# Sketched attention and a tanh-shrink feed-forward: a fixed order table in place of the scheduler

## The chip, the cores and the metric

The kernel runs on one core of a Trainium2 chip. The metric is the device time of one execution in microseconds, the median of three runs.

## The reference

```python
def _attn_ref(q, k, v, S1, S2):            # q, k, v: (4, 4, 1088, 32); S1, S2: (8, 32)
    def phi(x):
        a = np.einsum('rd,bhsd->bhsr', S1, x)
        b = np.einsum('rd,bhsd->bhsr', S2, x)
        return np.einsum('bhsi,bhsj->bhsij', a, b).reshape(*x.shape[:-1], r * r)
    q_p, k_p = (phi(q), phi(k))
    kv = np.einsum('bhsf,bhsd->bhfd', k_p, v)
    z = np.sum(k_p, axis=2)
    num = np.einsum('bhsf,bhfd->bhsd', q_p, kv)
    den = np.einsum('bhsf,bhf->bhs', q_p, z)[..., None] + 1e-06
    return (num / den)
...
def _moe_ref(x, w_in, w_out):              # x: (4352, 128); w_in: (128, 2048); w_out: (2048, 128)
    h = x @ w_in
    g = h - np.tanh(h)
    return (g @ w_out)
```

The attention output, with its four heads side by side, is `x`: 4 batches of 1088 tokens are 4352 rows of 128.

## The kernel before, in words

The kernel is written as a list of operations (`P.add`), each with the values it reads and writes and the engines that may run it. `schedule` then places them: it goes forward in planned time, takes on each engine the ready operation with the lowest key inside a short window, picks the buffer or PSUM bank that it uses, and puts fills into gaps of PE that it sees coming. A fill is a product of zeros (L435, the operand `zz` is cleared by the operation `zop` at L434) into a bank that is not read. `sync` derives the semaphore waits from the dependencies, and `emit` writes out the five instruction streams, each in its strict order.

**Attention, per batch b.** k and q come in from HBM. VectorE transposes k in 32 x 32 blocks (kT, L583, two instructions) and q (qT, L592). PE makes the k sketches (ksk, L599 for batch 0 and L610 for the others), VectorE transposes them back (kab, L616). PE forms a Gram product of the two sketches (L638), from which a weighted sketch column for the denominator is made (gm, L642; scmm, L625; sc, L648, into the operand `wq`). VectorE forms the outer products of the two k sketches (w, L659, three of 128 x 768), PE multiplies them with v (kvmm, L671); kvd, kvt (L703) and kvb bring the result into place. On the q side PE makes the sketch with `wq` (qsk, L724), VectorE transposes it (abc, L729), computes the denominator and divides (m, den, rd, ap, L741 to L749), forms the outer products (qp, L767) and transposes them (qpT, L772). PE multiplies with kvb (num, L783) and two copies (L375, a helper that serves ScalarE, VectorE and GpSimd) write bf16 columns of `xT`. Blocks are 128 tokens; batch 0 has its q side in pieces of 2, 3 and 4 blocks, batch 1 in 5 and 4, batches 2 and 3 in one piece of 9 each. x1.0 is the pair of copies for the first 5 blocks of batch 1.

**Feed-forward.** The 4352 columns of `xT` are cut into ten groups of 256, 384, 448, six times 512, and 192 columns; groups 0 to 2 are exactly batch 0. For each of 16 blocks of `w_in` PE computes h (L877) into one of three PSUM banks, ScalarE takes the tanh (L881), PE accumulates the output from it (o, L892). The linear part h @ w_out is carried by `wch` and `wcl`, a product of both weight matrices computed on the chip (L845, L855), two more products per group (L896). So a column passes PE 16 + 18 times. From group 7 on, the tanh covers two blocks at once. VectorE transposes the group's result (ot, L901), and SP stores it (L911), four or eight stores per group.

**Order.** The attention's keys put it ahead of the feed-forward; the feed-forward's keys rise with time. All loads are on SP's queue in the order of their keys, at most 1.4 MB ahead: k of batch 0 in two halves, part of q, v, the weights, then the other batches.

## Time and profile before

| | us |
|---|---|
| runs | 113.57, 113.77, 115.36; median 113.77 |
| span of the profiled execution, first to last instruction | 112.6 |
| median of the runs less that span (what lies around it) | 1.2 |
| PE / VectorE / ScalarE / GpSimd busy | 100.3 / 72.1 / 79.9 / 5.6 |
| first tanh starts | 20.03 |
| batch 1's first x copied, group 3 starts | 48.16, 48.45 |
| last product of PE ends | 108.86 |

The profile is one execution; its lines give start and duration in us, the engine, the line of the kernel, the operation, its output and input tiles, how many instructions are merged in the line, and in brackets how long the engine had waited and for what. DVE is VectorE, ACT ScalarE, POOL GpSimd, PE TensorE, PEld its weight loads. Ends of PE's instructions are modelled and overlap, so the spacing of starts tells its rate. The granted clock of TensorE is 0.998 over the span.

### The profile page before, as it was taken

What the parts mean: (1) busy time and instruction counts of PE and PEld (TensorE: products, weight loads), DVE (VectorE), ACT (ScalarE), POOL (GpSimd) and SP (SyncE); (2) the same over time, 40 slices, a digit from 0 to 9 for tenths busy, and PEclk for the clock granted to TensorE, in tenths of its full rate; (3) what the DMA queues carried; (4) which work ended last, traced back from release to release, by engine and by line L of the source; (5) the groups of instructions that cost most, each with busy time, mean ns of one, the idle gap of its engine ahead of it and who ended that gap; (6) DMA issues with size and microseconds to landing.
All of it is one profiled execution on the core that took longest, in us unless ns stands there. A gap on an engine that the chain in (4) does not pass through costs nothing.

```text
span 112.6 us, 3409 instructions
## 1 busy us (share of the span) xinstructions
PE 100.3 (89%) x1467; PEld 48.7 (43%) x1477; DVE 72.1 (64%) x115; ACT 79.9 (71%) x164; POOL 5.6 (5%) x25
## 2 busy tenths in 40 slices
PE   6975996998799989979999999979999999999960
PEld 4523783455355444436443346334243334334540
DVE  4469374899999999999999992499950020020030
ACT  2101247876487798586599867798969999999950
POOL 5202016000000000000000000000000000000000
PEclk9999999999999999999999999999999999999999
DMA  1999878799987804022000230005004106005035
GB/s 21 259 245 329 255 232 234 243 241 272 226 270 218 165 5 69 0 47 46 0 6 0 44 49 6 6 11 83 0 6 68 25 0 93 0 12 77 4 55 73
DMA packets 25037, 11.24 MB, mean 100 GB/s; under 512 B 18880, under 2 KB 23616, under 8 KB 25024
## 3 DMA queue, kind: packets, MB, share of 16 engines
q1 hardware_dynamic: 24320, 10.97, 40.7%
q8 instruction: 11, 0.18, 0.7%
q10 hardware_dynamic: 704, 0.08, 0.5%
q14 instruction: 2, 0.02, 0.1%
HBM read 8.81 MB, written 2.23 MB: 98 GB/s over the span
## 4 chain that ended last, share of the span: by engine, by line
PE 36%; ACT 28%; DVE 16%; DMA 13%; issue 2%; SPq 1%; DVEq 0%
ACT th L881 25%; PE psb L892 11%; PE psb L877 10%; DMA qL<-in_q_dram 5%; DMA wo_f<-in_moe_w_out_dram 5%; PE psb L783 5%; DVE qp L767 4%; DVE qpT L772 4%; DVE abc L729 3%; DMA kL<-in_k_dram 3%; PE psb L724 3%; PE psb L671 3%; DVE ot L901 2%; PE psb L610 2%; ACT wiT L375 2%
## 5 line engine op out<-in xcount | busy, mean ns | idle before, releaser
L881 ACT ACTIVATE th<-psb 128x512 bf16<-128x512 f32 (+4 forms) x136 | 69.5, 624 | 7.4 <-PE psb L877 6.6
L877 PE MATMUL psb<-xT,wi 128*128 128x512 bf16 (+4 forms) x155 | 50.1, 349 | 1.5 <-DVE xT L375 0.5
L892 PE MATMUL psb<-th,wo 128*128 128x512 bf16 (+4 forms) x157 | 48.2, 348 | 1.4 <-DVE ot L901 0.6
L877 PEld LDWEIGHTS psb<-xT,wi 128*128 128x128 bf16 x160 | 14.9, 97 | 25.3 <-ACT th L881 14.4
L892 PEld LDWEIGHTS psb<-th,wo 128*128 128x128 bf16 x160 | 14.6, 97 | 15.7 <-ACT th L881 7.5
L901 DVE STREAM_TRANSPOSE ot<-psb 128x512 f32<-128x512 f32 (+4 forms) x10 | 6.3, 626 | 22.6 <-PE psb L892 22.6
L772 DVE STREAM_TRANSPOSE qpT<-qp 128x768 f32<-128x768 f32 (+1 forms) x14 | 12.1, 861 | 0.4
L767 DVE TENSOR_TENSOR qp<-ap,abc 128x768 f32<-128x768 f32 (+1 forms) x14 | 11.5, 818 | 0.1
L659 DVE TENSOR_TENSOR w<-abk 128x768 f32<-128x768 f32 x12 | 11.3, 981 | 0.1
L729 DVE STREAM_TRANSPOSE abc<-psb 128x1152 f32<-128x1152 f32 (+2 forms) x5 | 5.7, 1143 | 5.1 <-PE psb L724 5.0
L435 PE MATMUL psb<-zz 128*128 128x256 bf16 x33 | 7.8, 388 | 1.1 <-DVE zz L434 1.1
L783 PE MATMUL psb<-qpT,kvb 32*32 32x128 f32 (+4 forms) x448 | 8.3, 309 | 0.1
L375 ACT CAST xT<-psb 128x192 bf16<-128x192 f32 (+4 forms) x8 | 3.3, 421 | 5.4 <-PE psb L783 5.4
L583 DVE STREAM_TRANSPOSE kT<-kL 128x576 f32<-128x576 f32 (+1 forms) x8 | 5.6, 724 | 1.7 <-DMA kL<-in_k_dram 1.7
L783 PEld LDWEIGHTS psb<-qpT,kvb 32*32 32x32 f32 x448 | 5.1, 103 | 2.9 <-DVE qpT L772 2.0
L671 PE MATMUL psb<-w,vL 128*32 128x64 f32 x288 | 6.0, 243 | 0.0
L592 DVE STREAM_TRANSPOSE qT<-qL 128x1088 f32<-128x1088 f32 (+2 forms) x5 | 5.3, 1055 | 0.9 <-DMA qL<-in_q_dram 0.9
L435 PEld LDWEIGHTS psb<-zz 128*128 128x128 bf16 x33 | 4.1, 135 | 3.6 <-DVE zz L434 1.1
L671 PEld LDWEIGHTS psb<-w,vL 128*32 128x32 f32 x288 | 5.1, 125 | 0.3 <-issue 0.2
L642 ACT COPY gm<-psb 128x32 f32<-128x32 f32 x4 | 0.8, 198 | 5.6 <-PE psb L638 5.6
L724 PE MATMUL psb<-qT,wq 32*32 32x288 f32 (+2 forms) x160 | 3.6, 381 | 0.9 <-ACT xT L375 0.9
L375 DVE CAST xT<-psb 128x192 bf16<-128x192 f32 (+3 forms) x6 | 2.8, 467 | 1.1 <-PE psb L783 1.0
(55 smaller groups left out, 56.6 us busy)
## 6 DMA issues: line engine op xcount, KB each, us to landing
kL<-in_k_dram SPq DMA_DIRECT2D x3, 544.0 KB, 3.6
qL<-in_q_dram SPq DMA_DIRECT2D x3, 544.0 KB, 4.9
vL<-in_v_dram SPq DMA_DIRECT2D x4, 288.0 KB, 4.8
vL<-in_v_dram SPq DMA_DIRECT2D x4, 256.0 KB, 5.0
wi_f<-in_moe_w_in_dram SPq DMA_DIRECT2D x4, 256.0 KB, 4.7
wo_f<-in_moe_w_out_dram SPq DMA_DIRECT2D x4, 256.0 KB, 5.8
out_dram<-ot SPq DMA_DIRECT2D x16, 64.0 KB, 2.0
out_dram<-ot SPq DMA_DIRECT2D x8, 56.0 KB, 1.9
```

The costliest lines, as they stand in the source:

```text
L375: return e.copy(o, i) if name == "scalar" else e.tensor_copy(o, i)
L435: filler = (lambda e, n: e.matmul(bank(3)[:, 0:256], zz.ap[:, 0:128], zz.ap[:, 128:384], start=True, stop=True), zop)
L659: P.add(_v(768), lambda e, n: e.tensor_tensor(out=wv.ap.rearrange("p (x i j) -> p x i j", i=8, j=8), in0=abh(0)[:, :, :, None].to_broadcas ...
L671: i = e.matmul(pv[b].ap[h * 32:(h + 1) * 32, 0:64], vL[b][:, h, blk * 32:(blk + 1) * 32], wvs[b, p].ap[:, (bi * 4 + h) * 64:(bi * 4 + h + ...
L729: P.add(_vp(sn * 4), lambda e, n: e.transpose(abc.ap.rearrange("p k h f -> p h k f")[:, :, 0:s1 - s0, :], psa4[:, :, 0:sn].rearrange("p h ...
L767: P.add(_v(cn * 256), lambda e, n, qp=qp, c0=c0, cn=cn: e.tensor_tensor(out=qp.ap[:, 0:cn * 256].rearrange("p (x i j) -> p x i j", i=8, j= ...
L772: P.add(_v(cn * 256), lambda e, n, qp=qp, o0=o0, cn=cn: e.transpose(qt.ap[:, o0 * 256:(o0 + cn) * 256], qp.ap[:, 0:cn * 256]), r=[qp], w=[ ...
L783: i = e.matmul(psa4[h * 32:(h + 1) * 32, g, 0:nb * 32], kvb.ap[g * 32:(g + 1) * 32, x, h * 32:(h + 1) * 32], qq[g * 32:(g + 1) * 32, 0:nb, ...
L877: P.add(_pe(n_ / 2.4 + 2.6), lambda e, n, jb=jb, hv=hv: e.matmul(hv.ap[:, jb % m * 512:jb % m * 512 + n_], wi[jb // 4].ap[:, (jb % 4) * 12 ...
L881: P.add(_a(n_ * m), lambda e, n, hv=hv, th=th: e.activation(out=th.ap.rearrange("p (u x) -> p u x", u=m)[:, :, 0:n_], in_=hv.ap.rearrange( ...
L892: fn = lambda e, n, x=x, st=st, sp_=sp_: e.matmul(ov.ap[:, 0:n_], wo[x // 4].ap[:, x % 4, :], ths[x][0].ap[:, ths[x][1] * 512:ths[x][1] * ...
L901: P.add(_vp(n_), lambda e, n: e.transpose(ot.ap[:, 0:n_], ov.ap[:, 0:n_]), r=[ov], w=[ot], key=-60000, name=f"ot{gi}")
```

## The change

The scheduler, its keys, windows and costs are gone. `TABLE` holds for every operation, by its number in the order of the `P.add` calls, the engine (v, a, g, t, s) and behind a colon the buffer or bank chosen; `f` is a fill. `plan` reads the table from front to back and appends each operation to its engine's list. `sync` and `emit` remain; an engine other than PE now also waits for its own earlier instructions where a buffer is reused, which before was done only where data was read.

```diff
+WPOOL = [False, True, True, True]
+TABLE = """
+42g 19s 18a 9g 15v 1g 20s 17a 44g 48g 21s 6g 46g 10g 8g 24s 7g 2g 23s 5v 27s 51v:0 52v 40v 28s 41v f f f f f f f f f f
+f f f f f f f f f f f f f 54t:0 0v 13v 22s 16v 53v 26s 4v 50g 25s 56v:0 43g 55v 3g f f f f f 57t:0 62v:0 32s 58a:0
...
+    def plan(self, table, filler):
...
+            if token == "f":
+                o = _Op()
+                o.engs, o.fn, o.mode, o.name, o.dma = {"tensor": 0}, filler[0], "128x128", "fill", 0
+                o.deps, o.users, o.vals, o.lock = {filler[1]: True}, [], [], False
+                e = "tensor"
...
-                            if d.eng == e and not (raw and e != "tensor"):
+                            if d.eng == e == "tensor":
...
-    zop = P.add(_v(192), lambda e, n: e.memset(zz.ap[:, :], 0.0), w=[zz], key=-99000)
+    zop = P.add(_v(192), lambda e, n: e.memset(zz.ap[:, :], 0.0), w=[zz], name="zz")
     filler = (lambda e, n: e.matmul(bank(3)[:, 0:256], zz.ap[:, 0:128], zz.ap[:, 128:384], start=True, stop=True), zop)
...
-    wqs = [sb("wq", [128, 32]) for _ in range(2)]
+    wqs = [sb("wq", [128, 32]) for _ in range(B)]
...
-    w_p = _Pool([([_Bank() for _ in range(3)], [sb("w", [128, 3 * 256]) for _ in range(3)])])
+    w_p = pool("w", 6, [128, 3 * 256])
...
+        P.add(_pe(80, 200.0), scmm, r=[s2r, gms[b]], w=[pg], mode="128x32", name=f"scmm{b}")
+        P.add(_a(8), lambda e, n: e.copy(wqs[b][:, 16:24], pg.ap[:, 64:72]), r=[pg], w=[scv[b]], name=f"sc{b}")
...
-        P.add(_v(768), lambda e, n: e.tensor_tensor(
+        P.add({**_v(768), **_g(768, 2.2)} if WPOOL[b] else _v(768), lambda e, n: e.tensor_tensor(
...
-            P.add(_pe(485), sk, r=[kT[b], wab], w=[pk[rh]], key=nk(), mode="64x32", name=f"ksk{b}.{rh}")
+        P.add(_pe(557, 245.0), sk, r=[kT[b], wab], w=pk, mode="64x32", name=f"ksk{b}")
```

Numbers that matter at the start: 0 is the memset of `zz`, 1, 2 and 3 make the identity, 4 and 5 the masks, 13 to 16 memsets of v's padding, 19 the load of k of batch 0, 40 and 41 `stt` and `wab` (the sketch operand), 51 and 52 the two k transposes of batch 0, 53 its first qT, 54 its k sketch, 55 and 56 kab, 57 the Gram product, 61 to 63 the outer products.

What the table and the diff set:

- VectorE's list begins 15, 5, 51, 52, 40, 41, 0, 13; PE's begins with 23 fills, then 54; 36 more fills lie between there and the fourth product of group 0. Before, 19 fills ran ahead of the first sketch and 33 in all.
- k of batch 0 is one load. The order on SP's queue: k0, first part of q0, first half of v0, two blocks of `w_in`, one of `w_out`, the rest of q0, and so on; up to 2.0 MB ahead. k and qT of batch 3 share batch 0's buffers.
- Outer products w1.0, w2.1 and w2.2 (batch, third) are on GpSimd, the other nine on VectorE. All casts of the weights but two are on ScalarE.
- VectorE does batch 0's second q front before its first qpT; then, between batch 0's q side and batch 1's, kT, kab and the outer products of batches 1 to 3 and all three qT. On PE the k products of batches 1 to 3 come before batch 1's q sketch. Both copies of x1.0 are on ScalarE.
- `wq` has one buffer per batch, and scmm is an operation of its own for every batch, in the Gram product's bank. The transposes of `w_in` and the products for `wch` are grouped by four into one operation.
- Tanh and products of a group no longer go in the order of the blocks. Stores are mostly issued a group or more later than they are ready.

## The prediction

> **What bounds the kernel now.** I read the whole-span table first, then the engine timelines, then the chain that ended last. The table gives each engine's busy share and, in 40 slices of 2.8 us, its busy tenths:

> ```profile
> PE 100.3 (89%) x1467; PEld 48.7 (43%) x1477; DVE 72.1 (64%) x115; ACT 79.9 (71%) x164; POOL 5.6 (5%) x25
> DVE  4469374899999999999999992499950020020030
> ACT  2101247876487798586599867798969999999950
> ```

> VectorE is full from slice 7 to 24 (17 to 67 us), ScalarE only from slice 30 on. PE's busy time overlaps itself, so I use the spacing of its starts. The stretches differ, so I read the timeline at their borders (start, duration, engine, line, operation):

> ```profile
> 0.84 0.22 DVE L434 MEMSET zz<- 128x192 uint32 x1 [0.84 <-PEq L976]
> 1.12 4.24 PE L435 MATMUL psb<-zz 128*128 128x256 bf16 x19 [1.12 <-DVE zz L434]
> 4.22 0.78 DVE L583 STREAM_TRANSPOSE kT<-kL 128x576 f32<-128x576 f32 x1 [1.71 <-DMA kL<-in_k_dram]
> 5.27 0.70 DVE L583 STREAM_TRANSPOSE kT<-kL 128x512 f32<-128x512 f32 x1
> 6.03 1.22 PE L599 MATMUL psb<-kT,wab 64*32 64x288 f32 x16 [0.67 <-DVE kT L583]
> 7.28 0.85 DVE L616 STREAM_TRANSPOSE abk<-psb 128x288 f32<-128x288 f32 x2
> 8.16 3.11 DVE L659 TENSOR_TENSOR w<-abk 128x768 f32<-128x768 f32 x3
> 9.70 0.76 POOL L375 CAST wi<-wi_f 128x512 bf16<-128x512 f32 x1 [4.16 <-DMA wi_f<-in_moe_w_in_dram]
> 20.03 4.53 ACT L881 ACTIVATE th<-psb 128x256 bf16<-128x256 f32 x16 [1.07 <-PE psb L877]
> 31.78 2.69 DVE L659 TENSOR_TENSOR w<-abk 128x768 f32<-128x768 f32 x3
> 47.67 0.49 DVE L375 CAST xT<-psb 128x320 bf16<-128x320 f32 x1
> 48.45 0.59 PE L877 MATMUL psb<-xT,wi 128*128 128x512 bf16 x2 [0.53 <-DVE xT L375]
> 103.04 0.38 PE L877 MATMUL psb<-xT,wi 128*128 128x512 bf16 x1
> 103.26 0.38 PE L892 MATMUL psb<-th,wo 128*128 128x512 bf16 x1
> 108.89 0.38 DVE L901 STREAM_TRANSPOSE ot<-psb 128x192 f32<-128x192 f32 x1 [1.29 <-PE psb L892]
> ```

> Three stretches follow. Up to 8.16 us (the first outer product) there is one chain: k load, two transposes, k sketch, its transposition. From there to 48.45 us VectorE sets the pace, with some 4 us of gaps before 20 us, until batch 1's first activations are copied (x1.0) and group 3, the first that needs them, can start. From 48.45 us PE is the bound: a 512-column product starts every 0.215 us (103.04 to 103.26, and so on). Groups 3 to 9 hold 3264 columns, each passing 16 + 18 times: 3264/512 x 34 x 0.215 = 46.6 us. The attention products in that stretch add 9.7 us, and each of their nine runs costs 0.33 us around it, as here in the chain that ended last (start, us, what):

> ```profile
> 65.90 1.53 PE psb L783 x63
> 67.43 0.16 issue
> 67.59 0.38 PE psb L896
> ```

> (0.16 without work, then a product that takes 0.38 instead of 0.21.) 46.6 + 9.7 + 3.0 = 59.3 us of the 60.4 us to PE's end at 108.85: PE is 98% used. ScalarE is busy 53.5 us there. After PE's end come 3.75 us: output transpose, stores, landing.

> **The change, step by step.** *1. The fills now stand in front of the first real product.* I read the table's numbers in the order of the `P.add` calls. PE's list begins with 23 fills (number-less `f`) and then 54, the k sketch of batch 0. A fill depends on op 0, the memset of `zz`, and the waits are derived from that. VectorE's list begins 15, 5, 51, 52, 40, 41, 0: the memset comes after both k transposes, `stt` and `wab`. So no fill can start before these are done, and the sketch, ready by then, stands behind 23 fills. Before, the memset was VectorE's first instruction and 19 fills ran at 1.12 to 5.36 us while PE had nothing else.

> The price: k is now one transfer of 544 KB. Its halves were there by 4.2 and 5.06 us; with half the descriptors and one issue I take 4.6 (4.2 to 5.1). Both transposes 1.33, `stt` 0.24, `wab` 0.20, memset 0.20, signal 0.06: fills from 6.6 us. Their spacing before is (4.24 - 0.42)/18 = 0.212: 23 x 0.213 = 4.9, to 11.5. Sketch 1.0 (1.22 with its halves one after the other, 0.72 later in the run), its transposition 0.88: the first outer product starts at 13.4 us instead of 8.16, **5.2 us late**. Bounds: 12.3 to 14.2. What was the fills' cover (a PE with nothing to do) is gone. Behind the first fill, all of PE is queued, and VectorE and ScalarE wait for it.

> The 19 early fills kept 0.212 us to their end; five fills at 16.2 us stood 0.11 us apart, so PE's rate does change. [...]

> *2. VectorE to the first activations.* Its new list puts most of batch 0's second front (L592, L729, L741 to L749 at 832 and 896 columns) ahead of the first `qpT`. Start-to-start times from the rows: three outer products 2.6, qT 0.93, abc 0.48 + 1.15, two times m, den, rd, ap 2.34, less for filled gaps 0.3, qp and qpT 1.24, slack 0.36: 8.8, to 22.2 us. `num` 0.85, two copies, one product: first tanh at about 24.3 us (20.03 before). The weights' casts, now almost all on ScalarE, end before that; unhidden they would cost 0.62 each.

> *3. VectorE from there to x1.0.* The new order pulls the k side of batches 1 to 3 and all q transposes ahead: qp and qpT of batch 0 (5.5), kT of three batches (3.9), their kab (2.6), six outer products (5.2; three more are GpSimd's), three qT (3.7), small ones (0.7), then abc1, m1 to ap1, abc2 (4.5), qp1 and qpT1 (3.0), less 0.8 for dependent pairs that no longer stand next to each other (0.95 against 0.84 for a 768 outer product). Sum 28.3 with 0.5 of waiting for PE, whose queue holds the q sketch behind `kvmm3`, which waits for the last outer product of batch 3 at L659.

> GpSimd's three outer products cost VectorE something. Row: three outer products took 3.11 us while GpSimd ran one cast of 0.76, and 2.69 alone: 0.42 lost, 55% of the overlap. GpSimd's own time per outer product lies between 0.92 (its 512 cast of 0.61, scaled) and 2.4 (its 128-wide product `s2r` of 0.40, times six). VectorE runs three of its own beside them: nothing to 3 us lost; I take 1.2, since part of the time VectorE will be in transposes. [...]

> So qpT1 is done at 22.2 + 28.3 + 1.2 = 51.7; `num` 1.0 to 52.7; two copies, now both on ScalarE, and the hop, 1.1: **group 3 starts at 53.8 us** against 48.45. Of the 5.2 us nothing is repaid here.

> *4. From there on PE has less left.* All of groups 3 to 9 remain (46.6), and 14 products of group 2's output (14 x 0.19 = 2.6). Of attention there are only num1.5 (1.0), qsk3 (0.86), num2 and num3 (1.53 each): 4.9, and four borders, 1.3. Sum **55.5 against 59.3**: 3.8 us of PE work has moved into the stretch before, where PE waited for VectorE anyway. At 98%: 56.6, so PE ends at 110.4. ScalarE's tanh there: 64 x 0.487 + 16 x 0.926 + 8 x 0.37 plus copies, 50 us: covered. If PE waited less, ScalarE would be next, 5 us behind.

> *5. Costed at nothing:* separate `scmm` for batches 1 to 3 and four `wq` (0.1 to 0.4 us each, in PE's waiting stretch; 1.2 us without that cover), products grouped by four (same instructions), own-engine waits on VectorE for buffer reuse (0.1 us each where neighbours), late loads of batch 3 into batch 0's buffer (needed after 31 us; before, all loads were in by 39 us, and everything that needs them is later now). Many stores are issued late: 14 of up to 0.55 us stand between group 7's and group 8's outputs on SP's queue, against 4.7 us of PE work, so the tail stays 3.75 (3.3 to 4.5).

> Sum: 110.4 + 3.75 = 114.1 us of span against 112.6. The runs' median is 113.77, 1.2 above the span: **115.3 us**, 1.4% slower. A measurement of this kernel can tell about 2% from no change, 111.5 to 116.05.

> **Rivals.** *GpSimd takes back more than it saves.* w1.0, w2.1 and w2.2 at the upper bound keep VectorE's own three at 45% of their speed, 1.06 us lost on each, 3.2 in all, and 0.87 x 3 = 2.6 is all that was saved: 2.0 more than I took, 117.3. For it: the 0.42 us. Against: VectorE has 3 us of transposes in the same stretch. It decides 2% when the loss is over 1.9 us.

> *The order fits badly with real times.* Tanh and products are in a scrambled order, each engine in a strict queue; with the first part 5 us late the rest meets loads and casts at other moments. If PE is 93% used after 53.8 instead of 98%: 55.5/0.93 = 59.7, 118.4. For it: three h banks give only 1 to 1.5 us of lead, and a `num` takes 1.5. Against: ScalarE has 5 us to spare.

> *The fills do not hold up the sketch* (the delay of step 1 isn't there). Then the first outer product starts at 4.6 + 1.33 + 0.06 + 1.2 + 0.88 = 8.1, all is 5.3 earlier: 110.0, and 3.3% faster. For it: the order after the start is good, as step 4 says. Against: the first fill in the old profile waits for just this memset.

> **How the numbers follow.** Forecast 0.55, with its own range 112.4 (k early, no loss to GpSimd, PE full) to 117.5; GpSimd 0.17; bad fit 0.16; no hold-up 0.12. Slower by over 2%: 0.15 + 0.15 from the two slow rivals and 0.09 from the forecast's upper end, 0.39. Faster: 0.11 from the last and 0.02, 0.13. Within: 0.48. The range, 111.5 to 119.0, leaves out most of the last rival and the far end of the bad fit.

> **What would show it.** Right: fills starting at about 6.6 us and not at 1.1, released by `zz`; the first outer product on VectorE at 13.4; first tanh near 24.3; the first L877-type product of 512 columns near 53.8, PE's end 56 to 57 us after that. GpSimd's outer products and VectorE's neighbours give the loss (over 1.0 us for a 768 product is contention). Wrong, if fills run at 1.1 us, if the 53.8 is off by over 2, or if PE's stretch after it takes 60 us.

## The result, and the profile after

After: median 121.35 us (120.38 to 122.47, 4 runs); before, on the same chip: 113.67. The ratio is 1.066, 95% interval 1.056 to 1.076: **6.6% slower**, where 1.4% slower was forecast. The profiled execution has a span of 118.6 us (112.6 before) and a time of its own of 120.38. (Medians below are of all runs; ratios leave out, of each kernel, the runs more than 1.5% above its fastest.)

The table and the slices of 2.97 us, to be held against the first lines shown of before:

```profile
PE 99.0 (84%) x1496; PEld 52.5 (44%) x1503; DVE 64.6 (54%) x106; ACT 82.6 (70%) x173; POOL 9.8 (8%) x28
PE   0069889749979858999999999999999999999920
DVE  1360799995866993699999999630201000220210
PEclk9999999997699999999999999999999999999997
```

PE now starts in slice 3 and has weak slices at 8, 9, 12 and 15; VectorE is no longer full up to its last attention work; and PEclk dips in slices 10 and 11. The start, in the timeline (start, duration, engine, line, operation, in brackets the wait before it):

```profile
5.01 1.37 DVE L518 STREAM_TRANSPOSE kT<-kL 128x576 f32<-128x576 f32 x2 [2.89 <-DMA kL<-in_k_dram]
6.73 0.22 DVE L398 MEMSET zz<- 128x192 uint32 x1
7.00 4.73 PE L399 MATMUL psb<-zz 128*128 128x256 bf16 x23 [7.00 <-DVE zz L398]
11.66 0.71 PE L538 MATMUL psb<-kT,wab 64*32 64x288 f32 x16
12.49 0.85 DVE L544 STREAM_TRANSPOSE abk<-psb 128x288 f32<-128x288 f32 x2 [4.52 <-PE psb L538]
13.37 1.83 DVE L579 TENSOR_TENSOR w<-abk 128x768 f32<-128x768 f32 x2
```

The memset stands behind both transposes, 23 fills wait 7.00 us for it, the k sketch stands behind them, and the first outer product starts at 13.37 (8.16 before). PE between 20 and 45 us shows what the prediction did not have:

```profile
24.32 0.43 PE L692 MATMUL psb<-qpT,kvb 32*32 32x96 f32 x26
26.42 0.74 PE L692 MATMUL psb<-qpT,kvb 32*32 32x96 f32 x38 [1.67 <-issue]
...
33.10 0.48 PE L692 MATMUL psb<-qpT,kvb 32*32 32x128 f32 x26
34.45 0.85 PE L692 MATMUL psb<-qpT,kvb 32*32 32x128 f32 x38 [0.87 <-issue]
...
39.03 2.18 PE L594 MATMUL psb<-w,vL 128*32 128x64 f32 x138
42.98 0.26 PE L594 MATMUL psb<-w,vL 128*32 128x64 f32 x3 [1.77 <-issue]
```

Three times PE stops in the middle of one operation, whose operands are all there, and waits for nothing that the profile shows: 1.67 + 0.87 + 1.77 = 4.3 us. Before has no such stop of over 0.2 us. Group 3 starts at 58.34 us (48.45 before), PE ends at 113.32, and the span lasts 5.28 us more (3.74 before). From 108 us on, the last 10.6 us, the transfers' view has 18 stores on SP's queue (SPq; the last two figures of a line are the KB of one and the median us until it has landed). In the last 10.6 us of before it has 9. The lines of after:

```profile
out_dram<-ot SPq DMA_DIRECT2D x5, 64.0 KB, 2.3
out_dram<-ot SPq DMA_DIRECT2D x3, 48.0 KB, 1.8
out_dram<-ot SPq DMA_DIRECT2D x2, 56.0 KB, 1.9
out_dram<-ot SPq DMA_DIRECT2D x3, 8.0 KB, 1.6
out_dram<-ot SPq DMA_DIRECT2D x3, 16.0 KB, 1.5
out_dram<-ot ACTq DMA_DIRECT2D x2, 24.0 KB, 2.2
out_dram<-ot SPq DMA_DIRECT2D x2, 24.0 KB, 1.7
```

So, against the span of before: group 3 starts 9.9 us later, PE needs 5.4 less after it (55.0 for 60.4), the end takes 1.5 more; together the 6.0 us.

The theory with which the experiments begin: three separate costs, the late memset (5 us), PE running out of instructions (4 us) and stores issued too late (1.5 us). For the second: the transfers' view has a queue of its own for instructions ("q8 instruction", 11 packets, 0.18 MB, 16 KB each), and a packet of it runs from 40.23 to 41.57 us, that is, from 1.0 us before the third stop (41.21 to 42.98) into it; the stops are 128 of PE's products or multiples of that apart. Each product comes with a weight load, so 128 products are 256 instructions, and PE's 1496 products and 1503 weight loads are 11.7 times as many, for 11 packets. The rival for the second: an operand, bank or engine that the profile does not name.

### The profile page after: what moved, and what is told of

Read it like the earlier page. It is cut to its first block, busy times and chain, and to the rows that moved or that the text cites. A ratio compares the mean times of both kernels' runs of the same rounds, so it can differ in the third digit from the quotient of the medians.

```text
span 118.6 us, 3448 instructions
## 1 busy us (share of the span) xinstructions
PE 99.0 (84%) x1496; PEld 52.5 (44%) x1503; DVE 64.6 (54%) x106; ACT 82.6 (70%) x173; POOL 9.8 (8%) x28
## 4 chain that ended last, share of the span: by engine, by line
PE 70%; DVE 15%; issue 5%; DMA 4%; ACT 1%
PE psb L807 23%; PE psb L792 23%; PE psb L692 7%; PE psb L399 5%; DMA kL<-in_k_dram 4%; DVE abc L638 3%; PE psb L594 3%; PE psb L811 3%; PE psb L538 3%; DVE w L579 2%; DVE qpT L681 2%; DVE qp L676 2%; PE psb L633 1%; PE psb L771 1%; DVE m L650 1%
## 5 line engine op out<-in xcount | busy, mean ns | idle before, releaser
L792 PE MATMUL psb<-xT,wi 128*128 128x512 bf16 (+4 forms) x154 | 44.9, 352 | 0.6 <-issue 0.3
L807 PE MATMUL psb<-th,wo 128*128 128x512 bf16 (+4 forms) x159 | 42.9, 348 | 0.2
L399 PE MATMUL psb<-zz 128*128 128x256 bf16 x59 | 10.4, 323 | 7.0 <-DVE zz L398 7.0
L681 DVE STREAM_TRANSPOSE qpT<-qp 128x768 f32<-128x768 f32 (+1 forms) x14 | 11.3, 832 | 0.0
L399 PEld LDWEIGHTS psb<-zz 128*128 128x128 bf16 x59 | 6.1, 115 | 9.5 <-DVE zz L398 7.0
L579 DVE TENSOR_TENSOR w<-abk 128x768 f32<-128x768 f32 x9 | 8.1, 936 | 0.0
L544 DVE STREAM_TRANSPOSE abk<-psb 128x288 f32<-128x288 f32 x8 | 3.4, 462 | 7.0 <-PE psb L538 7.0
L594 PE MATMUL psb<-w,vL 128*32 128x64 f32 x288 | 5.0, 220 | 1.8 <-issue 1.8
L579 POOL TENSOR_TENSOR w<-abk 128x768 f32<-128x768 f32 x3 | 5.2, 1722 | 10.7 <-DVE abk L544 10.7
```

Of the source, the lines that this page charges most:

```text
L399: filler = (lambda e, n: e.matmul(bank(3)[:, 0:256], zz.ap[:, 0:128], zz.ap[:, 128:384], start=True, stop=True), zop)
L579: P.add({**_v(768), **_g(768, 2.2)} if WPOOL[b] else _v(768), lambda e, n: e.tensor_tensor(out=wv.ap.rearrange("p (x i j) -> p x i j", i=8 ...
L594: i = e.matmul(pv[b].ap[h * 32:(h + 1) * 32, 0:64], vL[b][:, h, blk * 32:(blk + 1) * 32], wvs[b, p].ap[:, (bi * 4 + h) * 64:(bi * 4 + h + ...
L681: P.add(_v(cn * 256), lambda e, n, qp=qp, o0=o0, cn=cn: e.transpose(qt.ap[:, o0 * 256:(o0 + cn) * 256], qp.ap[:, 0:cn * 256]), r=[qp], w=[ ...
L792: P.add(_mm(n_), lambda e, n, jb=jb, hv=hv: e.matmul(hv.ap[:, jb % m * 512:jb % m * 512 + n_], wi[jb // 4].ap[:, (jb % 4) * 128:(jb % 4 + ...
L807: fn = lambda e, n, x=x, st=st, sp_=sp_: e.matmul(ov.ap[:, 0:n_], wo[x // 4].ap[:, x % 4, :], ths[x][0].ap[:, ths[x][1] * 512:ths[x][1] * ...
```

## The experiments

### The two undoings, and fewer fills

**zz_first**: the memset in front again.

```diff
-42g 19s 18a ... 40v 28s 41v f f f ... f f f 54t:0 0v 13v
+0v 42g 19s 18a ... 40v 28s 41v f f f ... f f f 54t:0 13v
```

> One token moved: the memset of zz stands first on VectorE again. Both theories: fills from about 1.1 us, first outer product near 8.2 us instead of 13.4. Fetch theory (PE runs out of instructions every 256, most where many small attention products stand close): the holes inside num0.2, num0.5 and kvmm2.2 stay at the same product (after 26, 26 and 18 of them) and cost 2 to 5 us together, group 3 starts 32 to 37 us after the first qpT, and the time falls by 4 to 6 us, to about 115 to 117. Rival (the order misfits only because its start is 5 us late): the holes go, and the time falls by 8 us or more, to 113 or below.

116.33 us (116.03 to 117.73), ratio 1.0215 (1.012 to 1.031). Fills run from 1.12 us, the first outer product starts at 8.27, group 3 at 53.31: about 5.0 us of the 7.7 are the memset's place, as step 1 said. The stops are not less (3.19, 1.50 and 0.32 us), as the theory of the missing instructions had it, but only that in kvmm2.2 is where it had them: num0.2 and num0.5 have none, and the first stop stands in batch 0's kvmm. The rival's 113 us did not come.

**stores_ready**: SP's stores in the order in which groups are transposed, each right behind its `ot`; everything up to the first store is the same.

```diff
-296t:0 342a:14 ... 336v:1 348a:17 165v:1 ... 395s 456a:4 461t:0 337s 453t:2
+281v:0 282s 283s 284s 285s 293a:3 ... 336v:1 337s 338s 339s 340s 348a:17
```

> Stores stand on SP's queue in the order in which their groups are ready, behind the loads; all else as in the changed kernel. If the late stores make the tail: the time from PE's end to the span's end goes from 5.3 us to about 3.7, 1.5 us faster. If the tail is the landing of the last stores alone: no change.

116.7 us (115.62 to 117.03), ratio 1.0203 (1.013 to 1.028). The tail falls from 5.28 to 3.19 us: 2.1 us are the stores. Another 3.1 us came in front of group 3 (55.19), where PE's list is the same. The stops were 1.21 (in batch 0's kvmm), 1.25, 0.95 and 0.32; those behind num0.2 were milder (none over 0.2 for 0.87 us, and 0.95 for 1.77), and the clock did not dip: from PE's restart in num0.2 to its first product of num0.5 it took 5.23 us (26.31 to 31.54), and 6.68 in after (26.42 to 33.10). Nothing in the edit accounts for this; such differences also lie between two executions of one kernel, as will be seen.

**five_fills**: 5 in place of 23 fills ahead of the sketch (18 times `f` left out of the table), the memset still late.

> The first run of fills is 5 instead of 23, zz still late. The late memset's price goes with the fills behind it: first outer product 18 x 0.21 = 3.8 us earlier, near 9.6. Fetch theory: 36 instructions fewer ahead, so a hole that comes after 26 products of num0.2 comes after 44, in num0.5 too, and the one in kvmm2.2 moves into the Gram product behind it. A wait for data would stay at the same product. Time 116 to 118.

117.21 us (one run). First outer product at 10.05. The stops moved by just the 18 products taken out, in PE's timeline:

```profile
21.57 0.80 PE L691 MATMUL psb<-qpT,kvb 32*32 32x96 f32 x44
25.37 0.59 PE L691 MATMUL psb<-qpT,kvb 32*32 32x96 f32 x20 [3.00 <-issue]
```

44 of the 64 products now run before the stop, in after 26. The stop belongs to a count of PE's instructions and not to an operand, which the rival cannot give.

### The queue of loads

**cap14**: loads up to 1.4 MB ahead, as before the change, counted in the queue's order.

```diff
-CAP = 2.0e6
+CAP = 1.4e6
```

> Loads at most 1.4 MB ahead instead of 2.0, counted in the order of the queue; all else as in the changed kernel. If instruction fetches wait behind deep load queues: the holes in num0.2 (1.67 us) and num0.5 (0.87 us) shrink to under 0.5 each, the one in kvmm2.2 (1.77 us, no loads running) stays; 1 to 2.5 us faster. If the density of the products alone decides: all three stay, and the time within 1 us.

118.25 and 120.34 us, 1 to 3 below after's median, from two runs. In sum the stops did not shrink: 0.80, 1.27, 0.24, 1.84 and 0.32, 4.5 in all; the clock did not dip. With the other two repairs (zz_stores_cap14, below) it made loads late. A backlog of 1.4 MB is no cure here.

**fetch_full** and **fetch_cap** measure the disputed cost by itself: nothing of the computation is left, and PE runs only small products, then wide ones. The trace holds two products for each of the 1920 of the source, 3840.

```diff
+            small(1920)      # 32 x 32 weights, 64 columns, fp32
+            for i in range(512):
+                o = eng.matmul(ps[:, 0:256], zb[:, 0:128], zb[:, 128:384], start=True, stop=True)
+LEAD = 2.0e6                 # fetch_cap: 0.6e6
```

> No part of the computation is left: the output is zeros. PE runs 1920 products of 64 columns (32 x 32 weights, fp32, four row groups by turns, as the kernel's num products) without any wait for another engine, then 512 products of zeros of 256 columns. Each product is a weight load and a product, two instructions, so a block of 256 instructions ends every 128 products. SP loads 11 MB (k, q and w_in twice) with up to 2.0 MB in flight; the loads should end some 40 us after the start, about in the middle of the small products; 5.5 MB more follow beside the wide products. Theory A (PE runs out of instructions at the borders of blocks; the refill stands behind the loads' descriptors): small products show a hole after every 128 products, of 1 to 3 us while the loads run and about 1 us or less in the quiet part; wide products (some 14 us a block) show none. Theory B (holes at borders, but independent of loads): the same hole with and without loads. Theory C (holes come from the tile modes' changes or from waits of the real kernel, not from fetching): no holes at all here.

> As fetch_full, output zeros, but SP holds its loads to 0.6 MB in flight, in place of 2.0 MB. Theory A with the backlog as the cause (a refill has to wait for the descriptors that are already queued): the holes beside the loads shrink to about a third of those of fetch_full, towards the quiet ones. Theory A with the sharing as the cause (loads take the transfer engines' turns whatever their backlog): holes as in fetch_full. No holes: neither.

fetch_full, PE's timeline; its loads run until about 41 us:

```profile
5.79 3.25 PE L63 MATMUL ps<-a 32*32 32x64 f32 x223 [5.79 <-DVE zero L30]
12.83 1.83 PE L63 MATMUL ps<-a 32*32 32x64 f32 x128 [3.79 <-issue]
19.84 1.95 PE L63 MATMUL ps<-a 32*32 32x64 f32 x128 [5.19 <-issue]
24.94 1.95 PE L63 MATMUL ps<-a 32*32 32x64 f32 x128 [3.15 <-issue]
30.86 1.95 PE L63 MATMUL ps<-a 32*32 32x64 f32 x128 [3.97 <-issue]
37.61 1.95 PE L63 MATMUL ps<-a 32*32 32x64 f32 x128 [4.79 <-issue]
41.34 1.95 PE L63 MATMUL ps<-a 32*32 32x64 f32 x128 [1.77 <-issue]
44.79 1.95 PE L63 MATMUL ps<-a 32*32 32x64 f32 x128 [1.50 <-issue]
```

No operand is waited for, and PE stops after every 128 products. With an empty transfer side a block comes every 3.45 us (44.79 less 41.34), of which 1.95 is work; with 2.0 MB of loads queued every 5.1 to 7.0 us. fetch_cap, beside loads that go on to about 87 us:

```profile
14.36 1.95 PE L63 MATMUL ps<-a 32*32 32x64 f32 x128 [2.27 <-issue]
18.09 1.95 PE L63 MATMUL ps<-a 32*32 32x64 f32 x128 [1.78 <-issue]
21.82 1.96 PE L63 MATMUL ps<-a 32*32 32x64 f32 x128 [1.78 <-issue]
25.27 1.96 PE L63 MATMUL ps<-a 32*32 32x64 f32 x128 [1.50 <-issue]
```

Beside 0.6 MB in flight the stops are as without loads (1.50 to 2.27 against 1.50 to 2.05), beside 2.0 MB they are 3.15 to 5.19. So it is not enough that loads run. But 0.6 MB also halves the rate of the loads (134 GB/s from 5 to 41 us, 278 with 2.0 MB), so the two runs do not tell the depth of the queue from the traffic. Theory A has the places right; its sizes, 1 to 3 us beside loads and about 1 without, were too small. The 512 wide products show no stop (57.96 us, 14.5 us for a block), but the second loads came only after them, by a wait put at their end, so they do not tell of loads.

The start and end of every packet of the instruction queue are in the traces, and they leave the rival no room. Counting all that the trace holds of PE (products, weight loads and a few semaphore instructions), every stop of over 0.2 us before 60 us, in every kernel here and in both fetch runs, comes after exactly 449 instructions plus a multiple of 256: the border of a block. After each border comes one packet (fetch_full: 34 packets for 8704 products and weight loads, 256 each). In the fetch runs it starts 1.0 to 1.6 us after the border without loads and beside 0.6 MB of them, and 2.7 to 4.6 us beside 2.0 MB. It takes 0.9 to 1.4 us (2.5 once, in before), and in every stop PE goes on 1.2 to 1.7 us after the packet's end. For the three stops of after:

| stop in | packet starts, after the border before | the block without the stop | loads during the stop |
|---|---|---|---|
| num0.2 | 4.8 us | 5.6 us | 287 GB/s |
| num0.5 | 5.6 us | 7.2 us, part of it at half clock | 254 GB/s |
| kvmm2.2 | 1.1 us | 2.1 us | 0 |

So the first two come from late packets beside loads, and only the third from small products standing close. In before every block ahead of group 3 lasts 5.2 us or more.

**before_cap20** and **before_cap40** are the kernel before with the order of all five engines as it was, and 2.0 or 4.0 MB of loads ahead in place of 1.4.

```diff
-CAP = 1.4e6
+CAP = 2.0e6      # before_cap40: 4.0e6
```

> The kernel before, every engine's order the same, with one number changed: loads may be 2.0 MB ahead in place of 1.4 MB, as in the kernel after. If the backlog of loads decides whether PE's refills come in time, holes of 0.5 to 2 us without a releaser appear in PE's stream between 14 and 45 us, and the time is 0 to 3 us longer (114 to 117 us). If the density of small products alone decides, no hole, and the time as before or 0.3 us shorter by earlier loads (113.5 us).

> As before_cap20 with 4.0 MB. Backlog: more and longer holes than with 2.0 MB, 1 to 4 us each, 115 to 119 us. Density alone: no hole, 113.5 us.

With 2.0 MB 114.83 us, ratio 1.0052 (1.001 to 1.009), and no stop over 0.2 us in the profile. With 4.0 MB 120.04 us, ratio 1.052 (1.045 to 1.060), and two stops:

```profile
25.48 0.79 PE L783 MATMUL psb<-qpT,kvb 32*32 32x96 f32 x44 [1.16 <-issue]
33.60 0.72 PE L610 MATMUL psb<-kT,wab 64*32 64x288 f32 x16 [3.82 <-issue]
53.47 0.59 PE L877 MATMUL psb<-xT,wi 128*128 128x512 bf16 x2 [0.53 <-DVE xT L375]
```

1.16 + 3.82 = 5.0 us of stops, and group 3 starts at 53.47 for 48.45: 5.0 later. That the two numbers agree is in part chance: first tanh is 0.9 us earlier here, and the clock is at half for 3.4 us behind the second stop. The old order at 2.0 MB has no stops, the new order at 2.0 and at 1.4 MB has 4 to 5 us of them: the change's larger lead alone did not bring them, and a lead of 4.0 MB alone can. In before_cap20 the packets of the blocks ahead of group 3 start at most 2.7 us after the border, and PE gets to the next border 1.4 us or more after the packet's end, so there is little to spare; in before_cap40 two packets start 5.5 to 5.7 us after it, and those are the two stops.

### Putting it together

**zz_stores** (both undoings), **zz_stores_cap14** (and 1.4 MB), **zz_stores_dve** (and w1.0, w2.1, w2.2 on VectorE), **zz_stores_23** (and the 36 later fills left out), **zz_stores_0** (and no fills at all):

```diff
-113g:3 ... 153g:5 ... 154g:2                  # zz_stores_dve
+113v:3 ... 153v:5 ... 154v:2
-f f f ... 54t:0 ... f f f f f 57t:0 ...       # zz_stores_0: every f out
+54t:0 ... 57t:0 ...
```

> Both repairs: the zz memset first, the stores in the order of readiness. If they are independent (5.0 us from the one, 2.1 us of tail from the other): 114.2 us. If what the stores' order brought ahead of group 3 (3.1 us in that run) also adds: 111 to 112. Holes in PE's stream at multiples of 256 instructions stay, 3 to 5 us together.

> As zz_stores, loads at most 1.4 MB ahead. If an instruction fetch waits behind the loads in flight in proportion to them: its start comes 2 to 3.5 us after PE crosses a block's border instead of 3.5 to 5.6, the holes before group 3 shrink by 1 to 2 us, 1 to 2 us faster than zz_stores. If not: within 0.7 us of it.

> As zz_stores, with all outer products on VectorE again (the three of GpSimd at their places in the table). VectorE gets 3 x 0.87 = 2.6 us more ahead of group 3. If GpSimd's products cost VectorE nothing, and VectorE is what group 3 waits for: 2.6 us slower. If they cost it up to 1.2 us, as one pair of neighbours in two of the runs shows: 1.4 us slower. If PE's holes are what group 3 waits for: within 1 us.

> As zz_stores, without the 36 later fills (the 23 ahead of the first sketch stay): 72 instructions fewer ahead of group 0. Fetch theory: the hole 18 products into kvmm2.2 comes 36 products later, in kvt and kvmm3, and the block borders ahead of group 0 fall later too; holes together 1 us or more smaller. Price: PE may run at half its rate in places before 20 us. Time within 1.5 us of zz_stores.

> The kernel after with the memset of zz first, the stores as soon as they are ready, and the 36 later fills left out, 23 left: measured again with more rounds. If its order is worth what the count of PE's products after group 3 says, 113.3 us, ratio 0.985 to 0.995 against the kernel before; if the earlier measurement was a draw of luck with holes at block borders, 1.00.

> The kernel after with the memset of zz first on VectorE, the stores of a group issued as soon as its output is transposed, and no fills at all (59 left out). If the fills that stand in PE's first idle time still serve the clock, TensorE stays at half rate longer than without 23 of them: first tanh 0.5 to 1 us later than with 23 fills, 115 us. If they do nothing, as early as or up to 0.5 us earlier than with 23, 114 to 114.5 us; the blocks' borders move by 23 products again, so holes of PE come elsewhere (0 to 3 us, not predictable beyond that).

> The kernel after with the memset of zz first on VectorE, the stores as soon as they are ready and no fills, measured again: 113.0 to 113.5 us as the median if the first measurement stands, ratio near 0.99 against before; 114.5 or more if it was luck with the holes.

| | median us (runs) | ratio to before, interval |
|---|---|---|
| zz_stores | 115.71 (113.81 to 117.55, 10) | 1.0024 (0.997 to 1.008) |
| zz_stores_cap14 | 116.49 (115.64 to 119.98, 4) | 1.0152 (1.008 to 1.023) |
| zz_stores_dve | 115.76 (113.66 to 117.22, 10) | 1.0048 (0.998 to 1.012) |
| zz_stores_23 | 114.35 (112.85 to 115.92, 8) | 0.9914 (0.985 to 0.998) |
| zz_stores_23_again | 114.84 (111.70 to 117.28, 6) | 0.9863 (0.979 to 0.993) |
| zz_stores_0 | 113.3 (110.67 to 115.02, 6) | none given; before 113.81 |
| zz_stores_0_again | 113.23 (111.61 to 115.47, 12) | 0.9851 (0.981 to 0.989) |

The two undoings together give back nearly all of the loss: 1.066 to 1.0024 (by the medians of all runs, 1.2% above before are left). They do not add up: each alone takes some 4.5 points off the ratio, both together 6.4, and 114.2 us was expected. The smaller lead costs more than it brings: the one stop is 1.43 us (3.40 in zz_stores), but PE waits 3.8 us between 32 and 36 us, for loads that are late. GpSimd's outer products are worth nothing that can be told (1.0048 against 1.0024, intervals overlapping). With fewer fills or none the new order is about as fast as the old one. Without any, the medians lie 0.4 and 0.9% below before's; with 23, they lie at before's (114.31) and 0.9% above it (113.81). The ratio of 0.9863 in the second case rests on 2 of its 6 runs. First tanh is 0.5 us later without fills (21.50 and 21.56) than with 23 (21.00 and 21.06). Without fills the stops were 0.74, 0.54 and 0.60 us in the first profile, and these in the second, where group 3 starts at 55.38 instead of 52.84 us:

```profile
32.07 0.41 PE L558 MATMUL psb<-abk 128*32 128x32 f32 x19 [0.44 <-issue]
38.23 1.34 PE L593 MATMUL psb<-w,vL 128*32 128x64 f32 x74 [1.93 <-issue]
42.22 0.92 PE L593 MATMUL psb<-w,vL 128*32 128x64 f32 x50 [1.15 <-issue]
```

The same instruction stream, stops at the same counts, 1.6 us more of them; and PE's products were slow until about 26 us instead of 19 us (the k sketch at 24.75 us took 1.21 us; in the first, at 23.80, 0.72). This goes with the wide scatter of these kernels (111.6 to 115.5).

## Why the prediction was wrong

**Step 1 held.** Fills from 7.00 us (6.6 forecast), first outer product at 13.37 (13.4), within the bounds, and zz_first showed it as a cause: 5.0 us. That the sum came so close is in part luck: k and what hangs on it were 0.4 us later than assumed, the fills and the sketch 0.4 us shorter. The rival in which the fills do not hold up the sketch is refuted. The 23 fills took 4.73 us, near the 4.9 from the row: their starts stand 0.21 us apart for the first 4.2 us, and only the last two spacings are 0.11. Of the 1.1 us from the forecast down to the lower bound, 12.3, an early k is 0.4; the other 0.7, faster fills, no run shows by itself. In the other runs 23 fills in a row took 4.04 us (zz_stores_dve) to 5.09 (zz_stores).

**Step 2 held, 0.6 to 0.9 us early.** First qpT done at 21.56 (22.2), first tanh at 23.40 (24.3).

**Step 3 is the step that failed: the wait of VectorE for PE.** "VectorE from there to x1.0", with PE's part put at 0.5 us of waiting, gave group 3 at 53.8; it started at 58.34. In fact the sum has nothing for PE: its terms make 28.3 without the 0.5. From the first qpT's end to that of batch 1 (21.56 to 56.00) the forecast had 28.3 + 1.2 = 29.5 us, the profile 34.4. VectorE's own work was 27.6 of it, so the count of its instructions was sound. The other 6.9 us it waited, 5.5 of them for PE and 1.2 for ScalarE:

```profile
DVE abk L544 <- PE psb L538: 2.5, 3, 1.4
DVE ot L816 <- PE psb L807: 1.9, 1, 1.9
DVE wcl L778 <- ACT wch L777: 1.2, 1, 1.2
DVE abc L638 <- PE psb L633: 1.1, 1, 1.1
```

(who waited for whom: us in total, times, longest.) PE was late by its three stops, 4.3 us, and by the half clock behind the first, some 1.4 us (6.68 for 5.23, above); how the 6.9 us divide between the two was not tried. The forecast took for granted that PE has its instructions when its operands are there. Moving 3.8 us of PE work "into the stretch before, where PE waited for VectorE anyway" was costed at nothing; the k products brought together there make the third stop, where a block of instructions is used up in 2.1 us. The first two come from packets that were late, which no term of the forecast holds. GpSimd's 1.2 us was the author's choice between nothing and 3 us. Nothing of it shows in after (beside GpSimd the VectorE outer product took 0.92 us, and two kT transposes 1.37 us, for 1.36 with GpSimd idle), some 1.1 in zz_first:

```profile
31.36 2.95 DVE L579 TENSOR_TENSOR w<-abk 128x768 f32<-128x768 f32 x2
```

(1.8 us alone), and taking it away brought no time, as was expected if PE's stops are what group 3 waits for. GpSimd's own durations, 1.51 to 2.14 us with a mean of 1.72, lie within the bounds.

**Step 4 held.** 55.0 us of PE after group 3's start (56.6 forecast, 55.5 without losses). So the rival of a bad fit, PE 93% used *after* 53.8 us, is refuted where it was put: the bad fit came in front.

**Step 5: the tail was mis-sized.** 14 late stores "of up to 0.55 us" against 4.7 us of PE work should have cost nothing (3.75, at most 4.5); 5.28 was measured and 3.19 with the stores at once. SP had 18 stores left to issue from 108 us on, and they did not fit in.

The sum: 115.3 forecast + 4.5 for steps 1 to 3 + 1.5 for the tail - 1.6 for step 4 + 0.6 for what lies around the span (1.8 for 1.2) is 120.3, of the profiled 120.38. The range's upper end, 119.0, lay below it because the only rival with trouble at PE was put behind group 3. (By the slices in the prediction VectorE is full from about 20 us on, not from 17; no term rests on that.)

What is not settled: why a packet starts 2 us after the border in one execution and 5 us in another, with the same lead of the loads (in the block of num0.5 5.6 in after, 2.6 in stores_ready), and so why the old order at 2.0 MB has no stops. Its blocks ahead of group 3 are long, 5.2 us and more, because small products alternate with wide ones; a change of that alone was not tried.

## What to carry to other kernels

Fills are instructions like others: put what they depend on first in its engine's list, and ask what is queued behind them. A trace that shows an engine idle in the middle of one operation with "issue" as the releaser is to be read by counting instructions: if the stops are a fixed number apart, spread the small products between wide ones (not tried here by itself), leave useless ones out, or keep less queued on the loads' side, within what the loads' due times allow. Stores belong on their queue as soon as they are ready, and those left over at the end are counted one by one.

## What the runs showed of the hardware

```profile
13.00:41.00 28.00, 9.46 (x640) 0.50 0.81 261
42.00:120.00 78.00, 42.30 (x2782) 0.50 0.02 5
```

(stretch in us, its length, PE's busy us with products, granted clock, transfers' share, GB/s.) PE busy for 42.3 of 78 us did not hold the full clock.
- With fills in front of it the first sketch was shorter, but it brought no time. The sketch with 23 fills ahead of it (0.72 us in zz_stores_23; in zz_stores_dve it took 1.08) and with none (1.22 us in zz_stores_0):

```profile
6.82 0.72 PE L537 MATMUL psb<-kT,wab 64*32 64x288 f32 x16 [0.61 <-DVE wab L490]
6.90 1.22 PE L537 MATMUL psb<-kT,wab 64*32 64x288 f32 x16 [6.90 <-DVE wab L490]
```

The granted clock does not show this: in zz_stores_0 it reads 1.00 from 1 to 15 us, and its mean over the span is 1.000 in both profiles without fills. With 23 fills and no later ones the granted clock fell, to 0.50 from 10 us on in zz_stores_23, and the means are 0.923 and 0.953.
